# A second Strassen pair for x, weight rounding one piece further ahead, and moved VectorE work in a gated recurrence with a maxout FFN

## The chip, the core and the metric

The kernel runs on one core of a Trainium2 chip. The core has a matrix engine (TensorE, PE in the profile, with its weight loads as PEld), a vector engine (VectorE, DVE), a scalar engine (ScalarE, ACT), a general engine (GpSimd, POOL) and an engine that issues most transfers here (SyncE, SP). The metric is the device time of one execution in microseconds. Three runs of the kernel before took 422.75, 422.34 and 420.17 us, median 422.34.

## What is computed

```
f = sigmoid(f_logit)                                  # B 4, H 8, S 768, D 48, all float32
state = f[t] * state + outer(k[t], v[t])              # per batch and head, over t
y[t]  = q[t] @ state
x = y as (B*S, H*D)                                   # 3072 tokens x 384
h = maximum(maximum(x @ w1, x @ w2), x @ w3)          # 384 x 768 each
out = h @ w_out                                       # 768 x 384
```

The four weights come as float64.

## The kernel before

**Units and groups.** 64 steps of two batches make a unit `u` of 128 tokens; there are 24 units, and four of them make a group `g` of 512 tokens. The recurrence is done in blocks. For one unit VectorE turns the gate (L296), runs two scans (L329 `r`, L347 `prod`), turns k and q (L296 `kt`, `qt`) and the keys (`keys_by_blocks(u, n)`, L382, four sets of four transposes, `ks`); GpSimd makes `ends` (L339), `kh` (L340), `qh` (L351) and the carried `state` (L357). TensorE does four bundles of small matmuls: `pairs(u)` (L392, reads kh and qh), `values(u)` (L411), `sums(u)` (L436, reads ks) and `finish(u)` (L500, reads qh and state, gives the x of the unit, transposed, in `xT`).

**Who orders the work.** The schedule is written out by hand: the loop over u at the end of `fast()` emits the parts of one unit, and between them calls `fill(ns)`, which takes steps from a generator (`ffn_first` for group 0, `ffn` for groups 1 to 5) until their stated cost has used up the budget. Each engine then runs its instructions in the order in which they were emitted, and waits where an operand is not there. All q, k, f and weight transfers are issued on SyncE in that order, too.

**Weights.** Each float64 piece of 128 x 384 (18 of w1, w2, w3, then 6 of `w_out`, numbers 0 to 23) is loaded as raw words and rounded to float32: `round_begin` on ScalarE (L240 to L244), `round_end` on VectorE (L254) and then GpSimd (L258). For w2 and w3 `apart` (L715) subtracts w1. So the FFN takes the maxima relative to x w1, `hm`, and the output is hm @ w_out + x @ w_lin, where w_lin = w1 @ w_out is made by `linear(a)` (L745, 18 matmuls of 384 columns) and spread to the padded layout of x by transfers in `place` (L454, L461), as w2 - w1 and w3 - w1 are in `placed`.

`ffn_first` has 18 steps for the inputs of group 0 (matmuls at L537, the maximum at L767). After step n it calls `round_to(ROUNDED[n])`, so `ROUNDED` says how many pieces are rounded by then. `linear` rounds one more piece for each of its yields, until all are done. Then come the outputs of group 0 (`outputs`, L563).

**Groups 1 to 5.** `inputs_by_pairs` (L836) computes the inputs with a Strassen-like scheme on two of three blocks of x; its last part, `fourth(2)`, ends with two maxima on VectorE (L886, L887) and `sums_of_hm` (L596) on GpSimd. `outputs_by_pairs` (its matmuls are all at L609) takes the six blocks of 128 of hm as three pairs: with halves of the tokens and halves of the 384 columns, seven products do the work of eight. The mixed weights `w_mix` are made by `mix(n)` on GpSimd (L587), the mixed sums of hm, `s1`, `s2`, `s4`, in `s_mix`. The three blocks of x against w_lin are done plainly, four places. That is 22 yields of three matmuls of 192 columns. The results gather in three PSUM banks, `a`, `b` and `c`: bank a goes through all of A00, s2, A01, X1, A11 and X1 again without being cleared, and is read by ScalarE between them (`read(b, n)`, L614, into `partial[n]`), b and c are added to such a part by VectorE (`add`, L617) and GpSimd (L662).

At the end come tests for values outside a range (L1092 to L1101) with a branch to a general version that is not taken here.

Of the kernel before, what the change touches and what calls it, by code (L numbers as in the profile page):

```python
# [55 lines left out]
def kernel(  # L56
# [33 lines left out]
    def fast():  # L90
        ctx = ExitStack()
        with ctx:
# [484 lines left out]
            w_mix = [keep.tile([128, HJ, HD], FP32, name="mix")] + [w_in[2][:, :, n * HD:(n + 1) * HD] for n in range(4)]  # L577
            s_mix = [w_in[1][:, n, :].rearrange("q (jj t) -> q jj t", jj=HJ) for n in range(NK)]
            partial = [w_in[0][:, n, 0:DM] for n in range(NK)]
            pairs_of = lambda t: t.rearrange("q (p c) -> q p c", p=2)  # L580

            def mix(n):

                dst, x, y = ((w_mix[2], corner(1, 1), corner(0, 1)), (w_mix[0], corner(0, 1), corner(0, 0)),
                             (w_mix[1], corner(1, 1), w_mix[0]), (w_mix[3], corner(1, 0), w_mix[1]),
                             (w_mix[4], w_lin[:, :, 0:HD], w_lin[:, :, HD:]))[n]
                nc.gpsimd.tensor_tensor(dst, x, y, op=ALU.subtract)  # L587

            def sums_of_hm(hm, jj):

                first, second = ([hm[:, 2 * jj + k].rearrange("q (p n t) -> q n p t", p=2, n=2)[:, n] for n in range(2)]
                                 for k in range(2))
                s1, s2, s4 = (pairs_of(t[:, jj]) for t in s_mix)
                for dst, x, y, op in ((s1, first[1], second[1], ALU.add), (s2, s1, first[0], ALU.subtract),
                                      (first[1], first[0], first[1], ALU.subtract), (s4, second[0], s2, ALU.subtract)):
                    nc.gpsimd.tensor_tensor(dst, x, y, op=op)  # L596

            def outputs_by_pairs(g, hm, xT):
                tile_of = lambda p, n: slice((2 * p + n) * UT, (2 * p + n + 1) * UT)
                A = lambda k, n: lambda p: hm[:, k::2, tile_of(p, n)]  # L600
                X = lambda n: lambda p: xT[:, 0:NK, tile_of(p, n)]
                s1, s2, s4 = (lambda p, t=t: t[:, :, p * UT:(p + 1) * UT] for t in s_mix)
                lin = [w_lin[:, :, n * HD:(n + 1) * HD] for n in range(2)]
# [3 lines left out]
                def into(b, p, lhs, rhs):  # L607
                    for k in range(HJ):
                        nc.tensor.matmul(b[:, p * HD:(p + 1) * HD], lhsT=lhs(p)[:, k], rhs=rhs[:, k],  # L609
                                         start=id(b) not in begun, stop=(k == HJ - 1), skip_group_check=True)  # L610
                        begun.add(id(b))
# [7 lines left out]
                COST = HJ * HD * COLUMN  # L619
                a, b, c = bank(), bank(True), bank(True)  # L620
                into(b, 0, X(0), lin[0])
                yield COST
                into(b, 1, X(0), lin[0])
                yield COST
                into(a, 0, A(0, 0), corner(0, 0))
                yield COST
                into(b, 0, A(1, 0), corner(1, 0))
                yield COST
                into(a, 1, A(0, 0), corner(0, 0))
                read(a, 0)  # L630
                yield COST
                into(b, 1, A(1, 0), corner(1, 0))
# [3 lines left out]
                yield COST  # L636
                into(a, 0, s2, w_mix[1])
                yield COST
                into(a, 1, s2, w_mix[1])
                read(a, 1)  # L640
                yield COST
                d = b if last else c
                into(c, 0, s1, w_mix[0])
# [4 lines left out]
                into(d, 1, s1, w_mix[0])  # L648
# [5 lines left out]
                into(a, 0, A(0, 1), w_mix[2])  # L654
                yield COST
                into(a, 1, A(0, 1), w_mix[2])
                yield COST
                into(a, 0, X(1), lin[1])
                yield COST
# [3 lines left out]
                if last:  # L663
                    store_part(g, 1, 1)
                yield COST
                into(c, 0, X(0), lin[1])
                yield COST
                into(d, 1, X(0), lin[1])
                yield COST
                into(a, 0, A(1, 1), w_mix[3])  # L670
                yield COST
                into(a, 1, A(1, 1), w_mix[3])
# [3 lines left out]
                into(a, 0, X(1), w_mix[4])  # L676
                yield COST
                into(a, 1, X(1), w_mix[4])
# [3 lines left out]
                yield COST  # L682
                into(c, 0, s4, corner(1, 1))
# [3 lines left out]
                into(d, 1, s4, corner(1, 1))  # L687
# [64 lines left out]
            ROUNDED = (5, 7, 8, 10, 10, 11, 11, 12, 12, 13, 14, 15, 16, 17, 18, 20, 21, 22)  # L752
            TURNED = {3: 0, 4: 1, 6: 2, 13: 3, 15: 4, 17: 5}

            def ffn_first(xT):
# [27 lines left out]
                made = iter([lambda n=n: mix_in(n) for n in range(4)] + [lambda n=n: mix(n) for n in range(5)])  # L783
                for i in range(GRP):
                    for n, cost in enumerate(outputs(hm, xT, i)):
                        if i or n:
                            next(made, lambda: None)()
                        if i == GRP - 1 and n == 1 and 1 in packed:
                            sums_of_x(1)
                        yield cost  # L790
# [33 lines left out]
            def inputs_by_pairs(g, hm, xT):  # L824
# [57 lines left out]
                def fourth(n):  # L882
# [5 lines left out]
                    sums_of_hm(hm, n)  # L888
                    yield COST
# [49 lines left out]
            PART = (33 * TOK + 22 * HJ * HD) * COLUMN / (5 * GRP)  # L939
# [4 lines left out]
            with tc.manual_schedule():  # L944
# [78 lines left out]
                for u in range(GRP, NU):  # L1023
# [24 lines left out]
                    if u + 2 < NU:  # L1048
                        load_v(u + 2)
                    if n < NU:  # L1050
# [6 lines left out]
                    keys_by_blocks(u, 3)  # L1057
# [293 lines left out]
```

## Time and profile before

| | before |
|---|---|
| runs, us | 422.75, 422.34, 420.17 |
| median, us | 422.34 |
| profiled execution, us | 422.56 |
| its span, us | 420.8 |
| mean granted TensorE clock | 0.992 |
| PE busy, us | 402.0 |
| DVE busy, us | 277.8 |
| POOL busy, us | 242.1 |
| ACT busy, us | 178.8 |

The profile is one execution. Its first part gives the busy time of each engine, its second the span in 40 slices with the busy tenths of each engine (9 is 90% or more). The chain of work that ended last is followed back from the last instruction. A group row names a source line, an engine, an operation with output and inputs, the count, the busy time, the mean length of one in ns, and the idle time of the engine before it with what ended it. In a timeline a row has start, length, engine, line and operation, and in brackets the idle time before it. A float32 matmul leaves two records. Times in rows are us from the span's start unless they are marked ns.

### The profile page before, as it was taken

How to read it: one execution, taken by the hardware profiler on the slowest of the kernel's cores; microseconds unless marked ns; L12 is line 12 of the kernel's file. 1: busy time of each engine (PE TensorE's matmuls, PEld its weight loads, DVE VectorE, ACT ScalarE, POOL GpSimd, SP SyncE). 2: the span in 40 equal slices, each digit the busy share in tenths (PEclk: the TensorE clock that was granted, in tenths of full speed). 3: DMA queues.
4: the chain of work that ended last, by engine and by line, in shares of the span. 5: the costliest groups of instructions: out<-in, count | busy, mean ns of one | idle time of the engine just before them, and what ended most of it. 6: DMA issues, size and time to landing. Idle time of an engine off the chain costs nothing.

```text
span 420.8 us, 11553 instructions
## 1 busy us (share of the span) xinstructions
PE 402.0 (96%) x4618; PEld 336.9 (80%) x4618; DVE 277.8 (66%) x549; ACT 178.8 (42%) x412; POOL 242.1 (58%) x266
## 2 busy tenths in 40 slices
PE   4978999799999999999999999999999999999995
PEld 3766764466668888998889988889988889988994
DVE  6996597977697799868889867889774730002300
ACT  2478677512204442425541444442254524577210
POOL 2189456842989676376586357576556960435600
PEclk9999999979999999999999999999999999999999
DMA  8989986786456774277635276634473010552012
GB/s 170 243 261 268 246 217 90 91 149 153 85 114 89 116 146 61 67 102 103 121 102 107 46 120 77 122 104 88 60 146 96 9 54 10 155 142 75 1 21 60
DMA packets 181562, 47.21 MB, mean 112 GB/s; under 512 B 160448, under 2 KB 179200, under 8 KB 181504
## 3 DMA queue, kind: packets, MB, share of 16 engines
q1 hardware_dynamic: 178032, 45.62, 53.1%
q10 hardware_dynamic: 3472, 0.81, 0.9%
q8 instruction: 37, 0.61, 0.6%
q14 instruction: 21, 0.17, 0.1%
HBM read 37.75 MB, written 4.72 MB: 101 GB/s over the span
## 4 chain that ended last, share of the span: by engine, by line
PE 87%; DVE 6%; issue 2%; POOL 2%; DMA 1%; ACT 0%; SPq 0%; DVEq 0%; POOLq 0%
PE p L836 19%; PE tr L836 16%; PE p L609 15%; PE tr L609 12%; PE p L563 6%; PE p L537 5%; PE p L745 3%; PE y L500 3%; PE y L411 3%; PE a L392 2%; PE y L436 2%; DVE r L329 1%; POOL w_in L258 1%; DMA f_ld<-in_f_logit_dram 1%; DVE kh L340 1%
## 5 line engine op out<-in xcount | busy, mean ns | idle before, releaser
L382 DVE STREAM_TRANSPOSE ks<-kh 32x128 f32<-32x128 f32 x256 | 77.3, 302 | 5.1 <-POOL kh L340 1.0
L836 PE MATMUL tr<-xT,placed 128*128 128x256 f32 x300 | 73.4, 385 | 0.0
L836 PEld LDWEIGHTS tr<-xT,placed 128*128 128x128 f32 x300 | 55.6, 190 | 9.1 <-ACT hm L844 1.4
L836 PE MATMUL p<-xT,placed 128*128 128x256 f32 x180 | 45.0, 381 | 0.0
L340 POOL TENSOR_TENSOR kh<-kt,r 128x512 f32<-128x512 f32 x18 | 31.9, 1772 | 11.8 <-DVE kt L296 11.8
L329 DVE TENSOR_TENSOR_SCAN r<-gate,from_one 128x520 f32<-128x520 f32 x24 | 33.2, 1384 | 7.7 <-ACT gate L308 4.6
L617 DVE TENSOR_TENSOR o<-tr,w_in 128x384 f32<-128x384 f32 (+1 forms) x11 | 5.7, 515 | 48.8 <-PE tr L609 43.5
L836 PEld LDWEIGHTS p<-xT,placed 128*128 128x128 f32 x180 | 33.8, 190 | 4.7
L537 PE MATMUL p<-xT,w_in 128*128 128x256 f32 (+1 forms) x108 | 33.9, 458 | 3.4 <-POOL w_in L715 2.2
L506 ACT COPY xT<-y 64x256 f32<-64x256 f32 (+1 forms) x60 | 22.1, 369 | 29.3 <-PE y L500 28.7
L596 POOL TENSOR_TENSOR w_in<-hm 128x256 f32<-128x256 f32 x15 | 10.9, 726 | 39.8 <-DVE hm L887 39.8
L854 POOL TENSOR_TENSOR hm<-hm,rest_bits 128x512 f32<-128x512 f32 x15 | 22.0, 1467 | 18.8 <-ACT hm L844 18.8
L347 DVE TENSOR_TENSOR_SCAN prod<-gate,from_inv 128x520 f32<-128x520 f32 x24 | 31.8, 1326 | 0.0
L836 PE MATMUL p<-w_in,placed 128*128 128x256 f32 x120 | 30.0, 379 | 0.0
L258 POOL TENSOR_TENSOR w_in<-top_bits,rest_bits 128x384 uint32<-128x384 uint32 x18 | 21.6, 1206 | 13.7 <-DVE top_bits L254 7.2
L537 PEld LDWEIGHTS p<-xT,w_in 128*128 128x128 f32 x108 | 19.5, 190 | 12.0 <-issue 6.2
L662 POOL TENSOR_TENSOR o<-top_bits,w_in 128x384 f32<-128x384 f32 x5 | 5.1, 1013 | 41.7 <-ACT w_in L614 41.7
L879 DVE TENSOR_TENSOR hm<-tr,hm 128x512 f32<-128x512 f32 x15 | 10.2, 681 | 28.5 <-PE tr L836 18.4
L614 ACT COPY w_in<-p 128x384 f32<-128x384 f32 x15 | 7.2, 479 | 47.3 <-PE p L609 47.3
L280 ACT ACTIVATE raw<-top_bits 128x384 f32<-128x384 f32 x48 | 25.2, 526 | 0.4
L836 PEld LDWEIGHTS p<-w_in,placed 128*128 128x128 f32 x120 | 22.8, 190 | 3.1
L395 DVE TENSOR_TENSOR at<-a,mask 128x512 f32<-128x512 f32 x24 | 16.5, 688 | 12.5 <-PE a L392 12.2
(155 smaller groups left out, 891.3 us busy)
## 6 DMA issues: line engine op xcount, KB each, us to landing
raw<-in_moe_w_dram SPq DMA_DIRECT2D x24, 384.0 KB, 4.1
v_ld<-in_v_dram SPq DMA_DIRECT2D x48, 96.0 KB, 3.3
placed<-in_moe_w_dram SPq DMA_DIRECT2D x12, 384.0 KB, 5.7
out_dram<-o SPq DMA_DIRECT2D x46, 96.0 KB, 2.2
placed<-in_moe_w_out_dram SPq DMA_DIRECT2D x6, 384.0 KB, 5.4
f_ld<-in_f_logit_dram SPq DMA_DIRECT2D x36, 64.0 KB, 2.6
k_ld<-in_k_dram SPq DMA_DIRECT2D x36, 64.0 KB, 2.6
q_ld<-in_q_dram SPq DMA_DIRECT2D x36, 64.0 KB, 2.5
```

Source lines behind the costliest of these rows:

```text
L258: nc.gpsimd.tensor_tensor(dst, by(top), by(rest), op=ALU.add)
L280: nc.scalar.activation(over, size, AF.Relu, scale=(-1 / HI_MIN, 1.0)[step - 1], bias=(1.0, -HI_END * (1 - 2.0 ** -24))[step - 1], accum_ou ...
L329: nc.vector.tensor_tensor_scan(r[:, 0:LEN][:, ::-1], flat(gate)[:, ::-1], flat(from_one)[:, ::-1], 1.0, op0=ALU.mult, op1=ALU.max)
L340: (nc.vector if u < BY_ROWS else nc.gpsimd).tensor_tensor(kh.rearrange("p h a t -> p a h t"), kt, by_batch(r[:, 1:LEN + 1].rearrange("p (x ...
L347: nc.vector.tensor_tensor_scan(flat(prod), flat(gate_tiles[u % 2]), flat(from_inv[u % 2]), 1.0, op0=ALU.mult, op1=ALU.max)
L382: nc.vector.transpose(ks[n * 32:(n + 1) * 32, :, par, e0:e0 + 32], kh[p0:p0 + 32, :, a, t0:t0 + 32])
L506: nc.scalar.copy(xT[o, :, t0 + a * C:t0 + (a + 1) * C], y[i, a, 0:HP * C].rearrange("p (h t) -> p h t", h=HP))
L537: nc.tensor.matmul(p if w < TOK else p.rearrange("p (two t) -> p two t", two=2), lhsT=w_in[i][:, kt, j * 128:(j + 1) * 128], rhs=x[:, t.st ...
L563: nc.tensor.matmul(p[:, 0:DM], lhsT=lhsT, rhs=rhs, start=(n == 0), stop=(n == NJ + NK - 1))
L609: nc.tensor.matmul(b[:, p * HD:(p + 1) * HD], lhsT=lhs(p)[:, k], rhs=rhs[:, k], start=id(b) not in begun, stop=(k == HJ - 1), skip_group_c ...
L836: nc.tensor.matmul(b[:, j * HALF:(j + 1) * HALF], lhsT=w[:, (2 * n + j) * 128:(2 * n + j + 1) * 128], rhs=x, start=begin and j == 0, stop= ...
L854: nc.gpsimd.tensor_tensor(out(n, 0), out(n, 0), first, op=ALU.add)
```

## The change

1. In `outputs_by_pairs` two of the three blocks of x become a fourth pair of the scheme (index `HJ`), with their own sums `s_of_x` and mixed weights `x_mix`; one block stays plain. A group has 7 x 4 x 2 + 4 x 2 = 64 matmuls of 192 columns where it had 66.
2. The sums of x are made by `sums_of_x_pair` on VectorE, four operations of 128 x 256 per group; the first two at the start of the outputs, the others at A00's second half. The differences of the rows of w_lin are made by `mix_x` on GpSimd, five of 128 x 192, in group 1's `fourth(0)` and `fourth(1)`.
3. `w_mix[0]` is written into the place of a quarter of `w_out`; so `mix(1)` to `mix(3)` come together in the last output of group 0. The old `mix(4)` (w_lin, 576 wide) is gone.
4. The order of the outputs is X0, then A00 and A10 for the pairs other than hm's last (`early`), then these with the last pair (`rest`), s1, s2, A01, X1, X0, A11, X with `lin_mix`, s4. `COST` and `PART` follow the new sizes.
5. `ROUNDED` has other numbers from the seventh on.
6. `keys_by_blocks(u, 3)` is emitted before `scan(n)` instead of after it and a `fill(part)`.

```diff
@@ outputs_by_pairs and what it uses
-            w_mix = [keep.tile([128, HJ, HD], FP32, name="mix")] + [w_in[2][:, :, n * HD:(n + 1) * HD] for n in range(4)]
+            w_mix = [corner(0, 1)] + [w_in[2][:, :, n * HD:(n + 1) * HD] for n in range(4)]
+            x_mix = [w_lin[:, 0, HD:]] + [w_mix[4][:, n] for n in range(2)] + [keep.tile([128, HD], FP32, name="mix")]
-            partial = [w_in[0][:, n, 0:DM] for n in range(NK)]
+            s_last = keep.tile([128, HALF], FP32, name="s_last")
...
-                             (w_mix[1], corner(1, 1), w_mix[0]), (w_mix[3], corner(1, 0), w_mix[1]),
-                             (w_mix[4], w_lin[:, :, 0:HD], w_lin[:, :, HD:]))[n]
+                             (w_mix[1], corner(1, 1), w_mix[0]), (w_mix[3], corner(1, 0), w_mix[1]))[n]
                 nc.gpsimd.tensor_tensor(dst, x, y, op=ALU.subtract)
 
+            def mix_x(n):
+
+                of = lambda k, c: w_lin[:, k, c * HD:(c + 1) * HD]
+                dst, x, y = ((x_mix[2], of(1, 1), of(0, 1)), (x_mix[0], of(0, 1), of(0, 0)),
+                             (x_mix[1], of(1, 1), x_mix[0]), (x_mix[3], of(1, 0), x_mix[1]),
+                             (w_mix[4][:, 2], of(2, 0), of(2, 1)))[n]
+                nc.gpsimd.tensor_tensor(dst, x, y, op=ALU.subtract)
+
+            def sums_of_pair(x0, x1, *sums, part=slice(0, 4), engine=nc.gpsimd):
+
+                first, second = ([x.rearrange("q (p n t) -> q n p t", p=2, n=2)[:, n] for n in range(2)] for x in (x0, x1))
+                s1, s2, s4 = (pairs_of(t) for t in sums)
+                for dst, x, y, op in ((s1, first[1], second[1], ALU.add), (s2, s1, first[0], ALU.subtract),
+                                      (first[1], first[0], first[1], ALU.subtract), (s4, second[0], s2, ALU.subtract))[part]:
+                    engine.tensor_tensor(dst, x, y, op=op)
+
+            def sums_of_x_pair(xT, n):
+                sums_of_pair(xT[:, 0], xT[:, 1], *s_of_x(xT), part=slice(2 * n, 2 * n + 2), engine=nc.vector)
+
+            def s_of_x(xT):
+                return [xT[:, NK, 0:HALF], xT[:, NK, HALF:TOK], s_last]
...
+                order = [*range(HJ - 1), HJ, HJ - 1]
+                A = lambda k, n: lambda p: [(xT[:, k] if jj == HJ else hm[:, 2 * jj + k])[:, tile_of(p, n)] for jj in order]
+                C = lambda k, n: [(w_lin[:, k] if jj == HJ else w_out[:, 2 * jj + k])[:, half(n)] for jj in order]
+                T = lambda i: [x_mix[i] if jj == HJ else w_mix[i][:, jj] for jj in order]
+                X = lambda n: lambda p: [xT[:, 2, tile_of(p, n)]]
+                partial = [w_nat[:, n, :] for n in range(NK)]
...
+                sums_of_x_pair(xT, 0)
                 into(b, 0, X(0), lin[0])
-                yield COST
+                yield PLAIN
                 into(b, 1, X(0), lin[0])
-                yield COST
-                into(a, 0, A(0, 0), corner(0, 0))
-                yield COST
-                into(b, 0, A(1, 0), corner(1, 0))
-                yield COST
-                into(a, 1, A(0, 0), corner(0, 0))
+                yield PLAIN
+                early, rest = slice(len(order) - 1), slice(len(order) - 1, None)
+                for p in range(2):
+                    into(a, p, A(0, 0), C(0, 0), early)
+                    if p:
+                        sums_of_x_pair(xT, 1)
+                    yield COST - PART_COST
+                    into(b, p, A(1, 0), C(1, 0), early)
+                    yield COST - PART_COST
+                for p in range(2):
+                    into(a, p, A(0, 0), C(0, 0), rest)
                 read(a, 0)
-                yield COST
-                into(b, 1, A(1, 0), corner(1, 0))
+                yield 2 * PART_COST
+                for p in range(2):
+                    into(b, p, A(1, 0), C(1, 0), rest)
                 add(o_of(0, 0), b, 0)
...
-                into(a, 0, s2, w_mix[1])
-                yield COST
-                into(a, 1, s2, w_mix[1])
-                read(a, 1)
-                yield COST
                 d = b if last else c
-                into(c, 0, s1, w_mix[0])
+                into(c, 0, s1, T(0))
...
-                into(d, 1, s1, w_mix[0])
+                into(d, 1, s1, T(0))
...
-                into(a, 0, A(0, 1), w_mix[2])
+                into(a, 0, s2, T(1))
                 yield COST
-                into(a, 1, A(0, 1), w_mix[2])
+                into(a, 1, s2, T(1))
+                read(a, 1)
+                yield COST
+                into(a, 0, A(0, 1), T(2))
+                yield COST
+                into(a, 1, A(0, 1), T(2))
                 yield COST
                 into(a, 0, X(1), lin[1])
...
-                into(a, 0, X(1), w_mix[4])
+                into(a, 0, X(1), lin_mix)
...
@@ ffn_first
-            ROUNDED = (5, 7, 8, 10, 10, 11, 11, 12, 12, 13, 14, 15, 16, 17, 18, 20, 21, 22)
+            ROUNDED = (5, 7, 8, 10, 10, 11, 12, 13, 14, 15, 16, 17, 18, 19, 20, 21, 22, 23)
...
-                made = iter([lambda n=n: mix_in(n) for n in range(4)] + [lambda n=n: mix(n) for n in range(5)])
+                made = iter([lambda n=n: mix_in(n) for n in range(4)] + [lambda: mix(0)])
...
+                        if i == GRP - 1 and n == 2:
+                            for k in range(1, 4):
+                                mix(k)
@@ inputs_by_pairs, fourth(n)
                     sums_of_hm(hm, n)
+                    if g == 1:
+                        for i in ((0, 1), (2, 3, 4), ())[n]:
+                            mix_x(i)
@@ the loop over units
-            PART = (33 * TOK + 22 * HJ * HD) * COLUMN / (5 * GRP)
+            PART = (33 * TOK + 64 * HD) * COLUMN / (5 * GRP)
...
+                    keys_by_blocks(u, 3)
                     if n < NU:
                         if n < BY_ROWS:
                             sigmoids(n)
...
                     fill(part)
-                    keys_by_blocks(u, 3)
                     if n < NU:
                         after(n)
                         before(n)
```

## The prediction

> **What bounds the kernel now.** I read the page's busy table first, then the chain that ended last, the list of waits, and at last the timelines where a wait stands.
>
> ```profile
> PE 402.0 (96%) x4618; PEld 336.9 (80%) x4618; DVE 277.8 (66%) x549; ACT 178.8 (42%) x412; POOL 242.1 (58%) x266
> PE   4978999799999999999999999999999999999995
> PE 87%; DVE 6%; issue 2%; POOL 2%; DMA 1%; ACT 0%; SPq 0%; DVEq 0%; POOLq 0%
> ```
>
> TensorE is busy for 96% of the span and is 87% of the chain; from the tenth slice (about 95 us) on every slice is full. So a matmul taken out there counts whole, and work on another engine counts only where TensorE comes to wait for it. The weight-load waits between 48 and 416 us that are not mere issue are few:
>
> ```profile
> PEld p L745 <- POOL w_out L258: 3.5, 2, 2.0
> PEld y L411 <- DVE kt L296: 1.3, 4, 0.3
> PEld p L609 <- DVE hm L886: 0.8, 3, 0.3
> ```
>
> The first is the rounding that the change moves. TensorE's timeline around it, and windows of 3.41 us laid against the clock (columns after the times: length, then TensorE's busy time, then PEld, DVE, ACT, POOL, the granted clock, the DMA share and GB/s):
>
> ```profile
> 77.71 1.45 PE L745 MATMUL p<-w_out,w_in 128*128 128x384 f32 x4
> 80.03 0.91 PE L745 MATMUL p<-w_out,w_in 128*128 128x384 f32 x2 [0.87 <-POOL w_out L258]
> 82.37 0.91 PE L745 MATMUL p<-w_out,w_in 128*128 128x384 f32 x2 [1.42 <-POOL w_out L258]
> 83.21 1.10 PE L500 MATMUL y<-qh,state 48*48 48x64 f32 x32
> 84.09 1.07 PE L392 MATMUL a<-qh,kh 48*64 48x64 f32 x32
> 85.10 7.83 PE L745 MATMUL p<-w_out,w_in 128*128 128x384 f32 x16
> 92.86 0.69 PE L411 MATMUL y<-at,v_ld 64*64 64x64 f32 x32
> ```
>
> ```profile
> 79.75:83.16 3.41, 1.71 (x4) 0.60 (x4) 3.31 (x8) 0.57 (x1) 2.01 (x3) 1.00 0.75 96
> 83.16:86.57 3.41, 3.41 (x68) 2.64 (x68) 2.88 (x7) 1.10 (x3) 2.13 (x2) 0.50 0.76 96
> 86.57:89.99 3.42, 3.42 (x7) 1.91 (x6) 3.25 (x7) 0.48 (x1) 0.19 (x1) 0.50 0.68 143
> 89.99:93.40 3.41, 3.41 (x45) 1.94 (x48) 1.85 (x3) 0.43 (x1) 3.14 (x3) 1.00 1.04 186
> ```
>
> Two waits, 0.87 and 1.42 us, leave TensorE half idle in one window; in the next two it is full but at half clock. Eight 384-column matmuls (two records each) take 7.83 us there; at 0.64 each, as three in 1.94 us in the chain at 98 us, they would take 5.15. With L500 and L392 (1.89 us here, about 1.1 elsewhere) the half clock costs 3.4 us.
>
> **The change part by part.** The sum stands against the profiled execution: span 420.8, 1.8 us around it, 422.56 us, 0.2 above the median of the runs.
>
> *Fewer matmuls.* A group from 1 on has 66 matmuls of 192 columns in its output; the scheme now takes 7 products of 4 blocks on two halves, 56, and 4 x 2 for the single x block: 64. That is 10 fewer in five groups.
>
> ```profile
> L609 PE MATMUL tr<-w_in,xT 128*128 128x192 f32 x120 | 21.1, 326 | 0.0
> ```
>
> Two records are one matmul. Twelve records in a row take 1.95 us in the chain at 161 us, so one matmul takes 0.325. TensorE is full here: **-3.25 us**.
>
> *Rounding ahead.* `w_out` pieces 20 to 23 reach GpSimd as follows (the last row is two pieces):
>
> ```profile
> 78.99 0.99 POOL L258 TENSOR_TENSOR w_out<-top_bits,rest_bits 128x384 uint32<-128x384 uint32 x1
> 81.33 0.99 POOL L258 TENSOR_TENSOR w_out<-top_bits,rest_bits 128x384 uint32<-128x384 uint32 x1 [0.56 <-DVE top_bits L254]
> 83.19 2.13 POOL L258 TENSOR_TENSOR w_out<-top_bits,rest_bits 128x384 uint32<-128x384 uint32 x2 [0.88 <-DVE top_bits L254]
> ```
>
> The change puts each L254 one or two steps earlier on VectorE, into 1.96 us that it stood idle before 71.3, and its L258 ahead of the attention of u=6 on GpSimd. With the same durations I walk the new order: piece 20 leaves GpSimd at 74.3, 21 at 78.8, 22 at 81.4, 23 at 83.5. TensorE then does four column blocks without a wait until 80.3, L500 and L392 until 81.4, the fifth block until 82.1, and waits 1.4 us (1 to 2) for piece 23. So 2.3 us of waiting become about 1.4. Carried on at full clock, L411 of u=6 starts at 88.1 instead of 92.9: **-4.8 us**, of which 3.4 is the clock, 0.9 the waits and 0.5 small gaps around them. Queued behind the earlier L258: `ends`, kh and qh of u=6 come 1 us later on GpSimd; L500, which needs qh, is not reached before 80.3, qh is done at 77.8.
>
> Here a rule speaks against the sum. The Trainium skill, page "TensorE: Matmul & The Clock Gate", section "Why this matters for your kernels", asks for gaps of no more than about 3 us between bursts, as one idle window brings the half clock back. By it, gaps of 0.87 and 1.42 us did nothing, the drop has another cause and stays, and this part is worth 1.4 us instead of 4.8. By the rows, the drop begins exactly where the emptiest window since 8 us (1.71 of 3.41 busy) ends, and it lasts two windows; 2.07 busy, at 8 to 11.5 us, had no drop. With one wait of 1.4 us a window has 2.0 busy: between the two, nearer the one without. I take the row; the same page says that the windows run free of the kernel, so a run may fall either way.
>
> *The lead's limit.* The transfers are issued in an unchanged order and without a pause from 71 to about 150 us, so they don't come earlier. The q of u=10 lands at about 136, its qh leaves GpSimd at 138.1, its reader L392 stood at 144.1; in the new order it stands 1 us earlier and leads by 4.8: 138.3. No wait, but nothing to spare: **+0.3** for it (0 to 1.5).
>
> *Output order.* The first group of output matmuls now leaves the last pair of hm to the end. At 163.2, 223.7 and 284.2 six records took 1.23 us instead of 0.97 for it, and there is a gap of 0.18 at 397: **-0.9**. In return A01 writes the bank that ScalarE has just read (copy 0.48, with signalling 0.75 us from the last matmul); before, other products stood between. L500 with L392 (1.1 us) cover it in groups 1 to 3, half of it in group 4, nothing in group 5: 0.2 + 0.75; the read before A11 is covered by two matmuls, 0.65 of 0.75, to 0.1 twice: **+1.1** (0.5 to 2). Without attention as cover it would be 0.75 in all five groups.
>
> *Sums of x on VectorE.* Four 128x256 operations of two SBUF inputs per group; the trace has none of that size. Nearest are the output adds:
>
> ```profile
> L617 DVE TENSOR_TENSOR o<-tr,w_in 128x384 f32<-128x384 f32 x9 | 5.0, 550 | 34.2 <-PE tr L609 28.8 <-ACT w_in L614 5.3
> L617 DVE TENSOR_TENSOR o<-tr,w_in 128x192 f32<-128x192 f32 x2 | 0.7, 358 | 14.6 <-PE tr L609 14.6
> ```
>
> Between them lies 0.42 us, 1.7 per group. But these read PSUM on one side. The Trainium skill, "SBUF — State Buffer", section "Who interferes with whom", says that a VectorE operation with two SBUF inputs and a GpSimd one that reads SBUF exclude each other. L715 on VectorE, two SBUF inputs, shows both: 0.55 us alone, 1.345 beside GpSimd. At that ratio it is 1.05 each, 4.2 per group. Two of the four are short of GpSimd's start (it waits 3.95 us for hm there), so I take the low end for them. *Transposes:* `ks` set 3 (four of 302 ns) moves ahead of gate and scan. Both stand in front of kt, prod and qt: 1.3 + 0.85 = 2.1 us later. Reader: in group 1 qh is done at 170.8, L392 starts at 173.9, 3.1 us of slack; elsewhere it is 4.9 to 6.1. In return ks is ready sooner for L436. Counted **0** (up to 1 us per group by the high end); with the cover gone every microsecond over 3.1 counts five times.
>
> *GpSimd.* One subtraction of 576 columns (1.40 us) goes, three others come in one burst (4.2 us) after group 0's last reads of `w_out`; they are done by about 130, thirty microseconds before their reader, and qh of u=10 behind them waits for q anyway. Five 128x192 in group 1, by the rows at 0.73 for 256 about 0.55 each, lie in idle stretches of 2.9 and 3.95 us before hm. Counted 0; uncovered it would be 2.8 once. Small: near 60 us gate and scan of u=5 come 0.9 us later behind the earlier L254, and TensorE reaches what needs them with little to spare, **+0.2** (0 to 0.9).
>
> Sum: -3.25 - 4.8 + 0.3 - 0.9 + 1.1 + 0.2 = -7.35, **415.2 us**.
>
> **Rivals.**
> *The half clock stays* (another cause, or the remaining wait falls into one window): 415.2 + 3.3 = 418.5 us. For it: the page's rule, and that 1.4 us are still waited. Against: the drop's place right behind the emptiest window.
> *The lead is lost to the side chain*: contended sums and q together cost 0.5 to 1 us per group, 418 to 420. For it: GpSimd's qh is the last link everywhere and has no slack at 138. Against: 3.1 us and more elsewhere.
> *Slower: VectorE becomes the bound in the output phase.* If the sums run at 1.05 and stretch GpSimd's kh (1.2 alone, 1.96 contended), qh is late by 1.3 + 2.1 + 1.5 + 0.8 = 5.7 us against 3.1 of slack: 2.6 us in each of five groups, 13 in all, 428 us. It decides from a delay of 3.1 us, and from about 5.4 the kernel is slower. Against: VectorE is 66% busy, and half of the sums stand behind the operations that qh needs.
> *No effect of the rounding* (GpSimd, not VectorE, holds the pieces): wait and clock as before, 422.56 - 3.25 + 0.2 = 419.5; part of the first rival's chance.
>
> **How the numbers follow.** Likeliest 415.2 (413 to 416.8): 0.66. Half clock stays: 0.20. Lead lost: 0.08. VectorE bound: 0.06. The likeliest's range with the first rival gives 412.9 to 419.3. About 1% is what a measurement of this kernel can tell from no change (the runs before spread over 0.6%), so the border is 418.1: 0.66 + 0.08 of the first rival + 0.03 of the second are faster, 0.77; 0.17 within; 0.06 slower.
>
> **What would show it.** Right: 64 matmuls of 192 columns per group at 325 ns; the L745 wait at one place, at or under 1.5 us, and 1.0 in all windows from 80 to 93; L411 of u=6 near 88; no L609 wait on hm, small ones on ScalarE L614 in groups 4 and 5; on VectorE the sums near 0.42. Wrong: a 0.5 in the clock row; L500 or L392 waiting for qh in the output phases; TensorE waiting on L351 near 138.

## The result and the profile after

Eight runs of each kernel gave a median of 417.68 us after the change (416.27 to 419.04) and 421.40 us before (420.12 to 423.83). The ratio is 0.9915, with a 95% interval of 0.9891 to 0.9940: a gain of 0.85%, about half of what was forecast. The profiled execution took 418.01 us (span 416.3) against 422.56 (span 420.8), 4.55 us less; the forecast's sum was 7.35.

The page of the changed kernel, busy times, the row of TensorE and the chain by engine:

```profile
PE 397.3 (95%) x4598; PEld 332.2 (80%) x4598; DVE 291.0 (70%) x569; ACT 178.5 (43%) x412; POOL 243.6 (59%) x270
PE   4978889999999999999999999999999999999995
PE 78%; DVE 8%; SPq 4%; DMA 4%; ACT 2%; POOL 2%; issue 2%; ACTq 0%; DVEq 0%; POOLq 0%
```

TensorE still bounds the kernel and is busy for 4.7 us less; the 20 records that are gone, ten matmuls, are 3.25 us of that. But the chain has lost 9 points of TensorE: VectorE, SyncE's queue and transfers stand in it now. Where the time went is read by stage, from the first matmul of each stage in the two timelines (us; positive is time lost):

| stage | before | after | difference |
|---|---|---|---|
| up to the first L537 | 25.29 | 25.69 | +0.40 |
| inputs of group 0 (`ffn_first`) | 52.42 | 54.08 | +1.66 |
| `linear` | 20.20 | 14.56 | -5.64 |
| outputs of group 0 | 28.29 | 28.29 | 0 |
| group 1, inputs | 34.90 | 35.31 | +0.41 |
| group 1, outputs | 25.51 | 25.38 | -0.13 |
| group 2, outputs | 25.51 | 24.61 | -0.90 |
| group 3, outputs | 25.51 | 24.61 | -0.90 |
| group 4, outputs | 23.06 | 23.27 | +0.21 |
| group 5, outputs | 21.98 | 22.35 | +0.37 |

The inputs of groups 2 to 5 differ by 0.01 at most. The whole is -4.53 at the last matmul. The +0.40 ahead of the first L537 is no effect of the change as far as the runs show: VectorE waited 0.49 us there for a weight transfer, and of two later runs of the changed kernel whose edits do not touch this part, one has its first L537 at 25.41 (s2 ahead of s1) and one at 25.71 (put together).

TensorE's timeline of the changed kernel, first near 60 us and then where `linear` (now L775) runs:

```profile
59.37 1.02 PE L537 MATMUL p<-xT,w_in 128*128 128x512 f32 x2
61.66 0.55 PE L767 MATMUL p<-ident,w_in 128*128 128x128 f32 x3 [1.26 <-DVE hm L797]
...
79.77 2.74 PE L775 MATMUL p<-w_out,w_in 128*128 128x384 f32 x8
82.44 0.66 PE L500 MATMUL y<-qh,state 48*48 48x64 f32 x32
82.93 0.65 PE L392 MATMUL a<-qh,kh 48*64 48x64 f32 x32
83.51 5.84 PE L775 MATMUL p<-w_out,w_in 128*128 128x384 f32 x16
89.28 0.69 PE L411 MATMUL y<-at,v_ld 64*64 64x64 f32 x32
```

In TensorE's own rows no wait is left at `linear`, and eight matmuls take 5.84 us and not 7.83. The list of weight-load waits from 76 to 96 us still has one, for piece 23:

```profile
PEld p L775 <- POOL w_out L258: 0.8, 1, 0.8
```

The L411 of u=6 starts at 89.28, 3.58 us earlier than before, not 4.8. The wait has moved: the transposes of w1 (L767) now stand at 61.66 and wait for VectorE's hm. Before the change they stood 2.0 us earlier without a wait, and the scan ahead of that hm began at 56.31:

```profile
59.65 0.49 PE L737 MATMUL p<-ident,w_in 128*128 128x128 f32 x3
56.31 1.88 DVE L329 TENSOR_TENSOR_SCAN r<-gate,from_one 128x520 f32<-128x520 f32 x1 [0.83 <-ACT gate L308]
```

Of the 2.0 us, 0.58 is there already at the L537 ahead of the wait (59.37, before 58.79). VectorE and then GpSimd of the changed kernel ahead of it:

```profile
54.48 1.32 DVE L254 SCALAR_TENSOR_TENSOR top_bits<-raw,top_bits 128x384 uint32<-128x384 uint32 x1
55.72 1.36 DVE L254 SCALAR_TENSOR_TENSOR top_bits<-placed,top_bits 128x384 uint32<-128x384 uint32 x1
57.98 1.35 DVE L745 TENSOR_TENSOR w_in<-w_in,w_in 128x384 f32<-128x384 f32 x1 [0.90 <-POOL w_in L258]
59.25 0.68 DVE L395 TENSOR_TENSOR at<-a,mask 128x512 f32<-128x512 f32 x1
59.85 1.22 DVE L329 TENSOR_TENSOR_SCAN r<-gate,from_one 128x520 f32<-128x520 f32 x1
61.11 0.21 DVE L332 RECIPROCAL from_inv<-r 128x8 f32<-128x8 f32 x1
61.23 0.37 DVE L797 SCALAR_TENSOR_TENSOR hm<-hm,p 128x256 f32<-128x256 f32 x1
```

```profile
54.37 1.01 POOL L258 TENSOR_TENSOR w_in<-top_bits,rest_bits 128x384 uint32<-128x384 uint32 x1 [0.56 <-DVE top_bits L254]
55.46 1.20 POOL L745 TENSOR_TENSOR w_in<-w_in,w_in 128x384 f32<-128x384 f32 x1
56.63 2.27 POOL L258 TENSOR_TENSOR w_in<-top_bits,rest_bits 128x384 uint32<-128x384 uint32 x2
```

Two more L254 stand ahead of the scan of u=5, beside GpSimd's L258 and L745, and each takes 1.3 us where one alone takes 0.55; then the subtraction L745 waits 0.90 for GpSimd and takes 1.35. The scan ends at 61.07, where it ended at 58.19.

**What the profile of before was.** The granted clock of each execution is known as a mean. In 59 executions of the kernel before, 36 have 0.996 or more, at a median of 420.25 us, 23 have 0.994 or less, at 421.39. The profiled one, with 0.992 and two windows at half clock, is of the smaller part; so the 3.4 us of the half clock, which the forecast took off, are not in most executions of before, and not in its median of 420.48. Of the 23, nine have 0.990 to 0.992, as the profiled one has, at a median of 422.96, which is 2.7 us above those at 0.996 or more; fourteen have 0.993 or 0.994, at 420.98. Two other sets of executions of before have 5 of 12 and 2 of 15 at 0.994 or less. In none of 14 executions of the changed kernel was the clock under 0.996. In the set with 5 of 12, the seven at 0.996 or more have a median of 420.46, and the changed kernel, run beside them, 417.27: at full clock on both sides the change gains 3.2 us, about what the ten matmuls are worth (3.25).

### The profile page after: what moved, and what is told of

It is laid out like the page before. It is cut to its first block, busy times and chain, and to the rows that moved or that the text cites. A ratio compares the mean times of both kernels' runs of the same rounds, so it can differ in the third digit from the quotient of the medians.

```text
span 416.3 us, 11545 instructions
## 1 busy us (share of the span) xinstructions
PE 397.3 (95%) x4598; PEld 332.2 (80%) x4598; DVE 291.0 (70%) x569; ACT 178.5 (43%) x412; POOL 243.6 (59%) x270
## 4 chain that ended last, share of the span: by engine, by line
PE 78%; DVE 8%; SPq 4%; DMA 4%; ACT 2%; POOL 2%; issue 2%; ACTq 0%; DVEq 0%; POOLq 0%
PE p L869 17%; PE tr L869 15%; PE p L631 14%; PE tr L631 11%; PE p L563 6%; PE p L537 4%; SPq L174 3%; PE y L411 3%; PE y L500 2%; PE p L775 2%; PE a L392 2%; PE y L436 2%; DMA raw<-in_moe_w_dram 2%; DVE ks L382 2%; DMA q_ld<-in_q_dram 1%
## 5 line engine op out<-in xcount | busy, mean ns | idle before, releaser
L339 POOL COPY ends<-r 128x8 f32<-128x8 f32 x24 | 8.6, 358 | 50.8 <-DVE r L329 50.8
L537 PE MATMUL p<-xT,w_in 128*128 128x256 f32 (+1 forms) x108 | 33.9, 458 | 3.4 <-POOL w_in L745 2.2
L329 DVE TENSOR_TENSOR_SCAN r<-gate,from_one 128x520 f32<-128x520 f32 x24 | 31.9, 1330 | 7.0 <-ACT gate L308 4.0
L340 POOL TENSOR_TENSOR kh<-kt,r 128x512 f32<-128x512 f32 x18 | 30.8, 1712 | 8.3 <-DVE kt L296 6.9
L537 PEld LDWEIGHTS p<-xT,w_in 128*128 128x128 f32 x108 | 19.5, 190 | 12.0 <-issue 6.2
L258 POOL TENSOR_TENSOR w_in<-top_bits,rest_bits 128x384 uint32<-128x384 uint32 x18 | 21.3, 1188 | 10.9 <-DVE top_bits L254 5.4
L631 PE MATMUL p<-w_in,hm 128*128 128x192 f32 x120 | 25.4, 335 | 1.1 <-ACT w_in L636 1.1
L631 PE MATMUL tr<-w_out,w_in 128*128 128x192 f32 x120 | 24.4, 326 | 0.0
```

Source lines behind the costliest of these rows:

```text
L258: nc.gpsimd.tensor_tensor(dst, by(top), by(rest), op=ALU.add)
L329: nc.vector.tensor_tensor_scan(r[:, 0:LEN][:, ::-1], flat(gate)[:, ::-1], flat(from_one)[:, ::-1], 1.0, op0=ALU.mult, op1=ALU.max)
L340: (nc.vector if u < BY_ROWS else nc.gpsimd).tensor_tensor(kh.rearrange("p h a t -> p a h t"), kt, by_batch(r[:, 1:LEN + 1].rearrange("p (x ...
L537: nc.tensor.matmul(p if w < TOK else p.rearrange("p (two t) -> p two t", two=2), lhsT=w_in[i][:, kt, j * 128:(j + 1) * 128], rhs=x[:, t.st ...
L631: nc.tensor.matmul(b[:, p * HD:(p + 1) * HD], lhsT=x, rhs=w, start=id(b) not in begun, stop=True, skip_group_check=True)
```

## The experiments

Intervals stand behind the ratios to the kernel before, run in the same set. "Lead" is how much earlier than in the profile of before a stage begins.

**Rounding undone.**

```diff
-            ROUNDED = (5, 7, 8, 10, 10, 11, 12, 13, 14, 15, 16, 17, 18, 19, 20, 21, 22, 23)
+            ROUNDED = (5, 7, 8, 10, 10, 11, 11, 12, 12, 13, 14, 15, 16, 17, 18, 20, 21, 22)
```

> The changed kernel with the old ROUNDED numbers. Theory (rounding ahead costs 2 us at 60 us and gives 5.6 us at 78 to 93): TensorE's wait for hm before the transposes near 60 us is gone, so L537 after them starts 2.0 us sooner, the waits on w_out near 80 us are back (about 2.3 us) and with them the half clock in two windows (3.4 us): the profile is 3 to 4 us slower than that of the changed kernel, about 421 to 422. Rival (the wait near 60 us comes from the moved ks transposes or the sums): that wait stays and the result is 5 us slower, about 423.

Median 418.84 us, ratio 0.9950 (0.9932 to 0.9968); the profiled execution took 417.65. Its timeline at `linear`:

```profile
80.02 0.91 PE L775 MATMUL p<-w_out,w_in 128*128 128x384 f32 x2 [0.87 <-POOL w_out L258]
82.36 0.91 PE L775 MATMUL p<-w_out,w_in 128*128 128x384 f32 x2 [1.43 <-POOL w_out L258]
83.20 0.66 PE L500 MATMUL y<-qh,state 48*48 48x64 f32 x32
```

The wait near 60 us is gone (`linear` begins at 77.69) and both waits at `w_out` are back, within 0.01 us, as the theory had it. But L500 takes 0.66 us: the clock stayed at 1.0 behind the same emptied window. So the half clock doesn't follow every time; 7 of 22 executions had 0.994 or less. The pair also gives its price: from L500 to the end of the stage this profile takes 11.94 us, and the profile of before 14.70, so the half clock cost 2.76 us there and not 3.4. At full clock the stage ends 0.8 us later than with the new numbers (95.14 against 94.33), and at the end the old numbers are 0.4 ahead (410.94 against 411.32): between these two profiled executions the new rounding gained nothing. The medians at a clock of 0.996 or more are 417.87 (15 executions, over a range of 1.6 us) and 417.37 (the 14 of the changed kernel, over 2.8), which doesn't settle whether it gains half a microsecond. The expected 3 to 4 us were wrong.

**Rounding ahead, but only behind the transposes.**

```diff
-            ROUNDED = (5, 7, 8, 10, 10, 11, 12, 13, 14, 15, 16, 17, 18, 19, 20, 21, 22, 23)
+            ROUNDED = (5, 7, 8, 10, 10, 11, 11, 12, 12, 13, 14, 15, 17, 19, 20, 21, 22, 23)
```

> The changed kernel with ROUNDED as before up to step 12 and two pieces more in steps 13 and 14, so (…, 11, 11, 12, 12, 13, 14, 15, 17, 19, 20, 21, 22, 23). Theory: no wait near 60 us, TensorE reaches the first w_out product 2 us sooner than in the changed kernel and then waits 1 to 1.5 us once; if the clock stays up, the lead at the L411 near 88 us is 4.5 to 5 us over before and the time is about 1 us under the changed kernel, less what the q transfers of u=10 give back: 416.5 to 418. Rival (a wait of 1 to 1.5 us is enough for the half clock): 3 us slower than that, about 420.

417.22 us, ratio 0.9906 (0.9876 to 0.9937).

```profile
77.80 2.10 PE L775 MATMUL p<-w_out,w_in 128*128 128x384 f32 x6
80.38 0.91 PE L775 MATMUL p<-w_out,w_in 128*128 128x384 f32 x2 [0.48 <-POOL w_out L258]
81.23 0.67 PE L500 MATMUL y<-qh,state 48*48 48x64 f32 x32
81.71 0.65 PE L392 MATMUL a<-qh,kh 48*64 48x64 f32 x32
82.72 0.91 PE L775 MATMUL p<-w_out,w_in 128*128 128x384 f32 x2 [0.37 <-POOL w_out L258]
84.59 4.78 PE L775 MATMUL p<-w_out,w_in 128*128 128x384 f32 x14 [0.95 <-POOL w_out L258]
```

TensorE arrives 2 us sooner and waits 1.80 us in three places; `linear` ends at 94.36 and in the changed kernel at 94.33. GpSimd's last row for `w_out` ends with piece 23. It is, in the changed kernel, here, and with the rounding undone:

```profile
83.52 0.99 POOL L258 TENSOR_TENSOR w_out<-top_bits,rest_bits 128x384 uint32<-128x384 uint32 x1 [0.88 <-DVE top_bits L254]
83.55 0.99 POOL L258 TENSOR_TENSOR w_out<-top_bits,rest_bits 128x384 uint32<-128x384 uint32 x1 [0.88 <-DVE top_bits L254]
83.18 2.14 POOL L258 TENSOR_TENSOR w_out<-top_bits,rest_bits 128x384 uint32<-128x384 uint32 x2 [0.88 <-DVE top_bits L254]
```

From the end of this row to the end of `linear` it is 9.82 us in all three. In five more profiles at full clock (the rounding alone, the wait filled, the changed kernel once more, s2 ahead of s1, put together) it is 9.81 or 9.82. That is the finding for this part: at full clock the stage ends a fixed time after piece 23 leaves GpSimd (84.51 us in the changed kernel, 85.32 with the rounding undone). A microsecond that TensorE saves near 60 is waited for here. No execution of six had a clock under 0.997. The one wait of 1 to 1.5 us came as three of 1.80 together, and the gain of 1 us was not there.

**The new rounding alone, in the kernel before.** The same line of `ROUNDED`, nothing else.

> The kernel before with the new ROUNDED numbers alone. Theory: the same 2 us wait near 60 us, no wait at w_out, no half clock, a lead of 3.6 us when L745 ends; nothing else changes, so 418.5 to 419 in the profile. Rival (half of the lead is given back at u=10 because the q transfers don't move): 420 to 421.

421.41 us, ratio 1.0012 (0.9988 to 1.0036): no gain. The profiled execution (419.67) shows the wait near 60 us (1.24) and a lead of 3.45 us behind `linear`, of which 2.87 are left when the outputs of group 1 begin. But 8 of 22 executions had a clock of 0.994 or less, at a median of 423.25, against 419.69 for the others. To see where the clock falls, it was run once more:

> The kernel before with the new ROUNDED numbers once more, to see where its clock falls. Theory (an emptied window near 20 to 30 us or near 60 us, where VectorE is late): a clock of 0.5 there in about two executions of five; elsewhere it is 1.0. Rival: the clock falls near 80 as in the kernel before.

419.92 us at a clock of 0.997, with no half clock to be seen. Where it falls in this kernel, and why not in the changed one with the same numbers, stays open: the emptiest windows of these two profiles after 8 us have TensorE busy for 1.92 and 1.96 of 3.41 us, hardly less than in the changed kernel's (1.96). So the gap near 80 us is not the only place where the clock of the old order of the outputs can fall.

**The wait filled.** The kernel before, with TensorE kept busy while it waits:

```diff
                 for j in range(NJ):
+                    for _ in range({2: 3, 3: 5}.get(j, 0) if a == 0 else 0):
+                        nc.tensor.matmul(p[:, DM:TOK], lhsT=ident, rhs=ident, start=False, stop=True,
+                                         skip_group_check=True)
                     nc.tensor.matmul(p[:, 0:DM], ...)
```

> The kernel before with eight dummy matmuls of 128 columns on TensorE (three before the third block of linear(0), five before the fourth), which fill 1.7 us of the 2.3 us that it waits for w_out there; they write a part of the bank that nobody reads. Theory (the half clock comes from the half empty window): the waits as seen by w_out stay, no window has a clock of 0.5, and L411 of u=6 starts 3 to 3.5 us sooner than before: 419 to 419.5 in the profile. Rival (the drop has another cause): clock 0.5 from 83 to 90 as before, 422 to 423.

Windows of 3.41 us (length, TensorE's busy time, then PEld, DVE, ACT and POOL, the clock, the DMA share and GB/s), before and then with the wait filled:

```profile
79.00:82.41 3.41, 1.12 (x4) 0.34 (x3) 3.29 (x8) 0.75 (x2) 2.76 (x4) 1.00 0.73 92
```

```profile
79.00:82.41 3.41, 3.02 (x20) 2.24 (x18) 3.28 (x9) 0.93 (x2) 2.85 (x4) 1.00 0.75 96
```

One of 22 executions had a clock of 0.994 or less, against 23 of 59 without the filling, in the same set: the emptied window does cause most of the half clocks of the kernel before. The theory stands there. Its gain doesn't: 420.57 us, ratio 1.0000 (0.9983 to 1.0016). At full clock it is 0.3 us slower than before (420.53 against 420.25). The dummies cost 0.2 us at `linear`, and the profiled execution, 2.6 us ahead when group 1 begins, takes 36.14 us for that group's inputs where the profile of before took 34.90. VectorE there waits 3.79 us for the q of u=10, and TensorE 0.5 us for GpSimd's sums of x (L823). So in this profile half of the lead is lost in group 1.

**The changed kernel once more**, for its clock:

> The changed kernel itself once more, for the granted clock of many executions. Theory (the half clock follows a window of 3.41 us in which TensorE is about half busy; here the emptiest is 1.96 us busy, in the kernel before 1.12): next to no execution has a clock of 0.994 or less, where the kernel before has it in 23 of 59; median 417 to 418. Rival (the half clock comes by chance): a share near 0.4 of the executions, median 418 to 419.

417.27 us, ratio 0.9910 (0.9880 to 0.9941); all six clocks 0.998 or more. In the two profiles of the changed kernel the emptiest window between 25 us and the last output, at 28.25, has TensorE busy for 1.96 of 3.41 us.

**Key set 3 back behind the scan.**

```diff
-                    keys_by_blocks(u, 3)
                     if n < NU:
                         if n < BY_ROWS:
...
                     fill(part)
+                    keys_by_blocks(u, 3)
                     if n < NU:
                         after(n)
```

> The changed kernel with key set 3 emitted after the scan again, as before. Theory (VectorE, 1.3 us later by the move, delays hm of the last pair and qh in group 1): the wait on hm in group 1's outputs (0.55 us) shrinks to 0.2 or less, and L436 waits for ks 0.3 us in some units instead; within 0.5 us of the changed kernel, profile 417.5 to 418. Rival (the move is what lets qh wait): 1 us or more faster.

Both were wrong: 430.82 us, ratio 1.0230 (1.0199 to 1.0261), 13.5 us slower than the changed kernel in the same set. Its waits of TensorE from 100 us on, and its timeline in group 2:

```profile
PE y L436 <- DVE ks L382: 8.7, 9, 2.1
```

```profile
228.26 0.69 PE L411 MATMUL y<-at,v_ld 64*64 64x64 f32 x32
228.78 0.27 PE L436 MATMUL y<-v_ld,ks 64*64 64x48 f32 x4
230.77 0.31 PE L436 MATMUL y<-v_ld,ks 64*64 64x48 f32 x2 [1.72 <-DVE ks L382]
231.43 0.66 PE L436 MATMUL y<-v_ld,ks 64*64 64x48 f32 x26 [0.34 <-DVE ks L382]
```

In the new order of the outputs L411 and L436 come 2.7 us after the start of a group's outputs, before the change 4.2 (165.34 less 161.10), and the sums of x now stand ahead of set 3 on VectorE. All five executions had a clock of 0.992 or less; in the profiled one the clock is 0.5 from 151.0 to 154.4 us and from 232.9 to 236.3, each time within 3 us after such a wait.

**The same without the sums of x.** `sums_of_x_pair` does nothing, and `s_last` is set to zero.

> The changed kernel with key set 3 after the scan again and the four sums of x left out (the output is wrong where they enter). Theory (the sums, 1.7 to 2.2 us of VectorE per group, push set 3 behind L436; it is the two together that cost 13 us): L436 waits for ks at most 0.3 us at a time, no half clock, 417 to 418. Rival (the late set 3 alone costs it in this order of outputs): L436 still waits, 420 or more.

423.81 us, ratio 1.0075 (1.0051 to 1.0100). L436 still waits for set 3, 4.2 us in eight places. So the rival is right as to the cause: the new order makes set 3 late by itself; the sums double it (8.7). The times are 7.0 us apart, more than the 4.5 us of waiting: all five executions with the sums had the low clock, and three of ten without them.

**Key set 3 moved in the kernel before.**

> The kernel before with key set 3 moved ahead of the scan, nothing else. Theory (before, set 3 is ready 0.15 us ahead of L436 in the output phases, so its place is no bound; qh has 3 us): no difference, 420 to 421. Rival (the move hides a wait that before has at L436): 0.5 to 1 us faster.

Again neither: 424.65 us, ratio 1.0112 (1.0075 to 1.0149), 4.6 us slower by the medians (420.06 before). The waits of TensorE from 100 us on, and the timeline at the start of group 1's outputs:

```profile
PE p L609 <- DVE hm L886: 4.5, 3, 1.5
```

```profile
160.22 0.81 PE L609 MATMUL p<-w_out,hm 128*128 128x192 f32 x4
162.53 0.59 PE L609 MATMUL p<-w_out,hm 128*128 128x192 f32 x2 [1.49 <-DVE hm L886]
```

Set 3 ahead of the scan makes hm's last pair 1.3 us late, and the old order reads it with the ninth matmul of a group's outputs. The order that reads it last and the moved set 3 need each other; either without the other is slower than the kernel before.

**The sums of x on GpSimd.**

```diff
-                sums_of_pair(..., part=slice(2 * n, 2 * n + 2), engine=nc.vector)
+                sums_of_pair(..., part=slice(2 * n, 2 * n + 2), engine=nc.gpsimd)
```

> The changed kernel with the four sums of x on GpSimd instead of VectorE. Theory (GpSimd makes kh and qh after the sums and has the less room): four of 0.73 us stand ahead of kh, VectorE's kt comes 0.9 us sooner; qh is about 2.5 us later in groups 1 to 3, L392 there waits 1 to 2 us each: 2 to 5 us slower than the changed kernel. Rival (the two engines exclude each other, so the place doesn't matter): within 0.5 us.

424.90 us, ratio 1.0086 (1.0056 to 1.0116): 7.6 us slower than the changed kernel in the same set, more than expected and by another wait:

```profile
PE tr L631 <- POOL xT L603: 5.0, 3, 2.2
```

Not qh comes late but the sums themselves, behind those of hm: TensorE stops in s1 for 2.2 us. The place does matter.

**s2 ahead of s1.** The two blocks of `outputs_by_pairs` exchanged:

```diff
+                into(a, 0, s2, T(1))
+                yield COST
+                into(a, 1, s2, T(1))
+                read(a, 1)
+                yield COST
                 d = b if last else c
                 into(c, 0, s1, T(0))
...
-                into(a, 0, s2, T(1))
-                yield COST
-                into(a, 1, s2, T(1))
-                read(a, 1)
-                yield COST
                 into(a, 0, A(0, 1), T(2))
```

> The changed kernel with the products of s2 ahead of those of s1, as before; so eight matmuls stand between the read of bank a and A01, and two between the first read and s2. Theory (bank a's read is what TensorE waits for in the last two groups): the wait of 0.57 us before A01 of group 5 goes, 0.1 us comes at s2 of groups 4 and 5; group 5's outputs take 22.35 - 0.7 = 21.6 us, the whole is 0.6 us faster. Rival (GpSimd has the last s2 of hm too late for the earlier place): 0.3 to 1 us of waiting for L603 in groups 1 to 3, no gain or slower.

416.89 us, ratio 0.9903 (0.9875 to 0.9930). Group 5's outputs take 21.77 us instead of 22.35, as expected; those of groups 2, 3 and 4 take 0.2 more each. The whole can't be told from the changed kernel.

**Put together.** Rounding late, but all of it done before `linear` (..., 14, 15, 17, 19, 20, 22, 23, 24), and s2 ahead of s1 in the last group only.

> The changed kernel with ROUNDED as before up to step 12, then 17, 19, 20, 22, 23, 24, so that all pieces are rounded before linear begins, and with s2 ahead of s1 in the last group alone. Theory: no wait near 60 us, none at w_out (or under 0.5), L745's part ends 1 to 2 us sooner than in the changed kernel; the q of u=10 lets at most about 4 us of lead through; the last group is 0.6 us shorter: 415.5 to 416.5. Rival (VectorE has keys and state of u=6 late behind the rounding): L411 or L436 near 90 us waits and the gain of the first part is gone, 417.

416.50 us (415.84 to 418.19), ratio 0.9908 (0.9875 to 0.9941). One wait of 1.11 us at `w_out` is left, where none or under 0.5 was expected, `linear` ends at 93.76, and the profiled execution took 415.84 us against 418.01. By the medians it is 0.8 to 1.2 us under the changed kernel, which its interval doesn't settle.

## Why the prediction was right in part

The sign and the wider range (412.9 to 419.3) held; the likeliest's own range (413 to 416.8) did not. The sum of -7.35 was 2.8 us too large, and the likeliest time 2.5 too low. The gain of 0.85% lies under the border of 1%, and to that side the forecast had given 0.17. That the range held is in part luck: its upper end stood there for a half clock that stays, and in the changed kernel none did. By its own steps, in the profiled execution:

**Fewer matmuls, -3.25.** Right. Groups 2 and 3, where the rows show no other wait of TensorE that changed, are 0.90 us shorter each: two matmuls, 0.65, and 0.25 of the wait for hm.

**Rounding, -4.8 with +0.2 near 60 us.** This is the step that failed, in two places. *The size of the wait near 60 us*: the forecast named the place and gave 0.2 (0 to 0.9) from a scan 0.9 us later; the scan was 2.9 later, and the transposes stand 2.0 later, 0.58 of it carried in from before 59 us. The 0.9 priced the added L254 at little more than its 0.55 alone, and left the subtraction's wait for GpSimd out. The contended row of L715 (1.345) was in the text, with the rule that the Trainium skill gives for it ("SBUF — State Buffer", section "Who interferes with whom"), but put to the sums of x alone; here, where GpSimd is busy with the same rounding, the added L254 took 1.32 and 1.36 us. *What the stage is bound by*: the walk had piece 23 leave GpSimd at 83.5; it left at 84.51, 0.8 us sooner than before and not 1.8, and at full clock the stage ends 9.82 us after it. Whatever TensorE wins near 60 it waits for at 84. The remaining wait of 1.4 us did appear, as 1.80, in the run with the late rounding.

**The half clock, 3.4 of the 4.8.** The place was right for the kernel before. By the rule that the forecast cites from the Trainium skill ("TensorE: Matmul & The Clock Gate", section "Why this matters for your kernels"), gaps of 0.87 and 1.42 us would not matter; filling them took the low clocks from 23 of 59 executions to 1 of 22, so the measurement decides against it here. Its weight was wrong twice. It is 2.76 us and not 3.4, as the forecast set eight matmuls at 5.15 us, and at full clock they take 5.74 (rounding undone), since TensorE then comes to piece 23 before GpSimd has it. And the profile of before was one of the executions that have it; its own time, 0.2 from a median of three, hid that. In most executions of before there was nothing to gain, and where filling gave a lead of 2.6 us, group 1 kept half.

**The lead's limit, +0.3.** Right in place and too small: 1.2 in all, inside its 0 to 1.5. Group 1's inputs lost 0.41. VectorE waited for the q of u=10 till 137.20, later than before (136.13), and from there it runs without a pause to the last pair of hm, which is done at 164.46 (before: 164.40). The rows, before and then after:

```profile
136.13 0.71 DVE L296 STREAM_TRANSPOSE qt<-q_ld 128x512 f32<-128x512 f32 x1 [0.51 <-DMA out_dram<-o]
163.71 0.69 DVE L887 SCALAR_TENSOR_TENSOR hm<-hm,top_bits 128x512 f32<-128x512 f32 x1
```

```profile
137.20 0.71 DVE L296 STREAM_TRANSPOSE qt<-q_ld 128x512 f32<-128x512 f32 x1 [2.04 <-DMA out_dram<-o]
163.78 0.68 DVE L920 SCALAR_TENSOR_TENSOR hm<-hm,top_bits 128x512 f32<-128x512 f32 x1
```

The brackets name a store, but the last of the q transfers is issued at 134.7 us and lands 2.4 us later, at 137.1. TensorE, 3.2 us ahead, waits for hm; so group 1's outputs gained 0.13 and not 0.90, as those of groups 2 and 3 did.

**Output order, -0.9 and +1.1.** The hm waits went in groups 2 and 3. The gap of 0.18 at 397 was misread: two one-column matmuls of the range test (L1099, L1100) stand in it, and they are still there at 391.66. The bank waits came to 1.8, with the 0.1 us by which the first matmuls after a wait are longer. In group 5 it is the uncovered read before A01, as forecast (0.73). In group 4 it is another: A11 was sized at 0.1, and waits because ScalarE's read stands behind a range test in its queue.

```profile
353.44 0.53 ACT L278 ACTIVATE top_bits<-raw 128x384 f32<-128x384 f32 x1
353.88 0.46 ACT L636 COPY w_in<-p 128x384 f32<-128x384 f32 x1
```

```profile
354.39 0.92 PE L631 MATMUL p<-w_in,hm 128*128 128x192 f32 x4 [0.54 <-ACT w_in L636]
...
401.12 0.92 PE L631 MATMUL p<-w_in,hm 128*128 128x192 f32 x4 [0.57 <-ACT w_in L636]
```

**Sums and transposes, 0.** Right as a total by luck, as the forecast had the reason upside down. VectorE's new group of rows:

```profile
L603 DVE TENSOR_TENSOR xT<-xT 128x256 f32<-128x256 f32 x15 | 9.6, 643 | 0.2
L603 DVE TENSOR_TENSOR s_last<-xT 128x256 f32<-128x256 f32 x5 | 3.1, 624 | 0.0
```

That is 2.5 us per group, between the 1.7 and the 4.2 given. The moved set 3 was counted as 1.3 us more of delay for qh. In the new order it is what keeps L436 from waiting: without it the kernel takes 431 us.

**The rivals.** "The lead is lost to the side chain" is what happened in group 1, together with the likeliest case. "VectorE becomes the bound" did not happen; the kernel with set 3 put back loses about its price, 13 us, but with ks and not qh as the late operand. "No effect of the rounding" is nearly true of the executions at full clock, where its effect is 0.5 us or less by the medians and not told from none.

## What to carry to other kernels

Before a stall in one profile is priced, ask how many executions have it: the runs' clocks or spread tell, and three runs do not. Where the engines that make an operand are late themselves, moving their work ahead may only move the wait of the engine that reads it; find the last link (here piece 23 on GpSimd) and price every moved instruction at the contended row where the other engine is busy. Parts of a change that look like separate costs can be each other's cover: the moved transposes lost 4.6 us alone and saved 13.5 in the new order.

## What the runs showed of the hardware

The half clock is a matter of chance even behind the same gap. The kernel before, with TensorE busy for 1.1 of 3.41 us in the emptied window, had a mean clock of 0.994 or less in 23 of 59 executions, and two profiles with the same waits (before, and rounding undone) differ in it. VectorE's L254, with two operands in SBUF, took 0.51 to 0.55 us alone and 0.91 to 1.37 us where GpSimd worked beside it. In the kernel with set 3 put back, two of three waits of about 2 us (1.90, 2.40 and 2.06 at L436) were followed by one window at half clock. TensorE had been busy for 1.72 and 1.80 of the 3.41 us ahead of these two windows. In the same steps of 3.41 us the longest wait falls mostly from 164.65 to 168.06, with TensorE busy for 1.55 us, and no drop followed. How empty a window must be can't be read from these runs.
